# Block 1's words loaded behind the rows of blocks 0 and 1, in a fused attention and expert kernel

## The chip, the cores and the metric

One core of a Trainium2 chip runs the whole program in one launch. The metric is device time in microseconds, the median of several executions. Matmuls run on TensorE, elementwise work on VectorE (DVE in the profile), ScalarE (ACT) and GpSimd (POOL); SyncE (SP) issues most transfers, GpSimd the indirect ones.

## The reference

Three stages, all in float32. An attention with decaying state runs over 4 batches, 8 heads, 768 steps and heads of 48. Its output, as 3072 rows of 384, goes to a layer of 8 experts; each row takes one of them. A dense layer of width 2048 with a squared relu follows.

```python
for t in range(S):
    cur = np.einsum('bhd,bhe->bhde', u[None] * kt, vt)
    y[:, :, t] = np.einsum('bhd,bhde->bhe', rt, state + cur)
    state = wt[:, :, :, None] * state + np.einsum('bhd,bhe->bhde', kt, vt)
...
e_idx = np.argmax(x @ w_gate, axis=1)
for e in range(E):
    mask = e_idx == e
    h = np.maximum(x[mask] @ w1[e], 0.0)
    out[mask] = gate_w[mask, None] * eom[mask, e, None] * (h @ w2[e])
...
g = np.maximum(x @ w_in, 0.0) ** 2
return g @ w_out
```

## The kernel before, in words

The attention works in 16 units (a batch and a pair of heads each). A unit's result `xT` is turned back into rows (`back`, two halves). When a batch is complete, a generator `route_steps` routes its 768 rows in small steps that are woven between other work: logits on TensorE, the choice of an expert on VectorE, ranks, a row `dsi` of destinations, and six indirect scatters by GpSimd that put the rows, sorted by expert within the batch, into the DRAM table `x_rows`. The last batch's steps are the `route_step()` calls. When all is routed, `finish_routing` sorts the experts by their number of rows and sets where each block finds its rows.

The experts' work is cut into blocks of fixed capacity. Block A holds the first 320 rows of expert 0 from the first three batches, so it can start before the last routing. Block 0 holds the rest of expert 0 (128 rows). Blocks 1 to 7 hold the other experts, the fullest first (480, 440, ... rows). A block gathers its rows (`gather`, one indirect DMA of GpSimd for each 128), multiplies them by the gate (`scale`), turns them (`prep_x`), and then goes through eight steps `f` of `up(f)` and `down(f)`. Every float32 factor is split into a high and a low part, and each product takes three matmuls. `prep_w(f)` splits step f's slices of `w1` and `w2` (the words): the high part by ScalarE, the low part by VectorE or GpSimd. The words come in two halves of four steps, 768 KB each for `w1r` and `w2r`, by `load(0)` and `load(1)` on SP, into two buffers that all blocks share. `put_ids` writes the rows' token numbers, 4 bytes each, into the DRAM list `x2_ids`; `put` and `put_A` write a block's result. `convert_load` fetches words of the dense layer, which VectorE converts (`convert_1`, `convert_2`).

Inside a `manual_schedule` each of the named engines keeps the written order. Two such parts stand one behind the other before the branch, and a planner may interleave them; a third stands behind the branch, in which GpSimd's order is the planner's. The branch (`tc.If(rare > 0)`, line 939) leads to work for inputs that the fast path can't hold; here it isn't taken, but each engine waits there for the transfers that it has under way.

What the change touches, in order of time: the end of the attention (`prep_x` of block A and the last unit's `back`), the steps of block A before the branch (`prep_w(FA)`, where FA = 4 is its fifth step, and `prep_w(FA + 1)`), block 1's `load(0)`, issued before the branch, and behind the branch the order of block 0's and 1's gathers, `put_ids`, loads and `convert_load(0)`. Block 0 works with block A's words. Lines 334 and 336 are the high and low parts of the splits, 330 and 331 those of `up`, 341 to 343 the three matmuls, 397 the gather, 242 the scatter, 477 and 481 `put_ids`, 321 and 322 the loads of words, 427 the transposes of `prep_x`.

Of the kernel before, what the change touches and what calls it, by code (L numbers as in the profile page):

```python
# [9 lines left out]
F32 = mybir.dt.float32  # L10
# [11 lines left out]
def rwkv_moe_kernel(  # L22
# [15 lines left out]
    nc = tc.nc  # L38
    B, H, S, D = r.shape
    NT, DM = out.shape  # L40
    E, _, F = w1.shape
# [6 lines left out]
    KD = DM // 128  # L48
# [4 lines left out]
    FA = 4  # L53
# [262 lines left out]
    rawctx = ExitStack()  # L316
    raw = rawctx.enter_context(tc.tile_pool(name="raw", bufs=2))

    def load_expert(pool, w1e, w2e, hf, into=None):
        t, t2 = into or (pool.tile([128, KD, F // 2], F32, name="w1r"), pool.tile([128, KF // 2, DM], F32, name="w2r"))  # L320
        nc.sync.dma_start(t, w1e.rearrange("o (c p) f -> p (o c) f", p=128)[:, :, hf * (F // 2):(hf + 1) * (F // 2)])
        nc.sync.dma_start(t2, w2e.rearrange("o (c p) d -> p (o c) d", p=128)[:, hf * (KF // 2):(hf + 1) * (KF // 2)])
        return t, t2
# [43 lines left out]
    class Block:  # L367
# [14 lines left out]
        def rows(self, i):  # L382
            return min(128, self.cap - 128 * i)

        def words_of(self, e):
            self.w1e, self.w2e = (t[ds(e, 1)] for t in (w1, w2))

        def load(self, hf, again=False):
            self.w1r[hf], self.w2r[hf] = load_expert(self.P.raw, self.w1e, self.w2e, hf, (self.w1r[hf], self.w2r[hf]) if again else None)

        def gather(self, tiles=None):
            one = self.nt == 1
# [5 lines left out]
                                             in_offset=IndirectOffsetOnAxis(ap=self.gcol(n, i), axis=0))  # L398

        def scale(self, eng=None):  # L400

            if self.ids is None:
                self.ids = self.P.xb[0].tile([128, NTL], F32, name="xid", bufs=3)
            for i in range(self.nt):
                n = self.rows(i)
                x, gate = self.xg[:n, i, :DM], self.xg[:n, i, DM:DM + 1]
                if eng:
                    eng.tensor_scalar(x, x, gate, None, op0=ALU.mult)
                else:
                    nc.scalar.activation(x, x, AF.Copy, scale=gate)  # L410
            i, n = divmod(self.cap, 128)
            for ids, num in ([(self.ids[:, :i], self.xg[:, :i, DM + 1])] if i else []) + \
                            ([(self.ids[:n, i:i + 1], self.xg[:n, i, DM + 1:DM + 2])] if n else []):
                if eng:
                    eng.tensor_copy(ids, num)
                else:
                    nc.scalar.copy(ids, num)
# [130 lines left out]
    def block_of(P, k, e):  # L548
        we = [t[e:e + 1] if isinstance(e, int) else t[ds(e, 1)] for t in (w1, w2)]
        return Block(P, CAPS[k], *we, lambda n, i: gi[:n, k, i:i + 1], (k + 1) % 2)  # L550
# [4 lines left out]
    def column(t, k):  # L555
        return nc.values_load(t[0:1, k:k + 1], engines=(ET.SP,), min_val=0, max_val=NCOL - 128 if t is offA else NT)

    def expert_of(k):
        return nc.values_load(bei[0:1, k:k + 1], engines=(ET.SP,), min_val=0, max_val=E - 1)
# [10 lines left out]
    def route_step():  # L570
        return next(routing[B - 1], 0)

    with ExitStack() as actx:
# [302 lines left out]

        blkA = first["A"]
        blkA.ps_w, blkA.w_names = ps_t, ["pt"] * KD
        blkA.prep_x(0)
        route_step()  # L880
        blkA.prep_x(1)
        blkA.prep_x(2)
        route_step()
        units[-1].back(0)
        units[-1].back(1)
        vs = cst.tile([128, 1], F32, name="vs")
        nc.vector.tensor_reduce(vs, viol, axis=AX.X, op=ALU.add)
        pf = ps_t.tile([128, 512], F32, name="pt")
# [6 lines left out]
    def put_ids_A():  # L895
        own = []
        for i in range(blkA.nt):
            n = blkA.rows(i)
            ins = nc.sync.dma_start(x2_ids[ds(column(offA, i) if i else 0, n)], blkA.ids[:n, i:i + 1])
            for o in own:  # L900
                tc.declare_no_dep(ins.ins, o.ins, reason="columns of their own")
            own.append(ins)

    with tc.manual_schedule(engines={ET.PE, ET.DVE, ET.Activation, ET.SP, ET.Pool}):
        put_ids_A()
        route_step()
        route_step()
        blkA.up(0)
        route_step()
        route_step()  # L910
        route_step()
        blkA.prep_w(FA, nc.vector)
        blkA.up(1)
        nc.vector.tensor_scalar(flag[:, 0:1], pf[:1, :1], 0.0, None, op0=ALU.is_le)
        blkA.down(0)
        more = None
        while more is None:
            nc.gpsimd.memset(warm, 0.0)
            more = route_step()
        tc.mark_branch_hint_location("rare", "LikelyTaken", [ET.PE, ET.DVE, ET.SP])  # L920
        finish = finish_routing()
        next(finish)
        blkA.prep_w(FA + 1, nc.vector)
        for f in range(2, FA):
            blkA.up(f)
            if f == 2:
                next(finish)
                next(finish)
                blk1 = block_of(P, 1, expert_of(1))
                blk1.load(0)  # L930
            blkA.down(f - 1)
        for _ in finish:
            pass
        blkA.down(FA - 1)
# [4 lines left out]
    with tc.If(rare > 0, label="rare"):  # L939
        fine = nc.values_load(flag[0:1, 0:1], min_val=0, max_val=1)  # L940
        with tc.If(fine == 0):
# [57 lines left out]
                    route(b, xT, xr, fk, ps_x, True)  # L999
            for _ in finish_routing():  # L1000
                pass
            blk1.words_of(expert_of(1))
            blk1.load(0, True)
            blkA.ps_w, blkA.w_names = ps_x, ["px"] * KD
            blkA.again(FA)
            put_ids_A()
# [61 lines left out]
    def convert_load(n):  # L1068
        f, which = divmod(n, 2)
        q = cv.tile([128, KD, 128, 2], I32, name="cq", bufs=3)  # L1070
        if which == 0:
            nc.sync.dma_start(q.rearrange("p c f o -> p c (f o)"),
                              w_in32.rearrange("(c p) f -> p c f", p=128)[:, :, f * 256:(f + 1) * 256])
        else:
            nc.sync.dma_start(q.rearrange("p c f o -> p (c f o)"), w_out32[f * 128:(f + 1) * 128])
        converted[n] = [q.rearrange("p c f o -> p (c f) o")]
# [117 lines left out]

    with tc.manual_schedule(engines={ET.PE, ET.DVE, ET.Activation, ET.SP}):
        block_rows()
        blocks = [block_of(P, 0, 0), blk1]
        blk0 = blocks[0]
        blk0.w1t, blk0.w2t = blkA.w1t, blkA.w2t
        blk0.gather()  # L1200
        atA = [column(offA, i) if i else 0 for i in range(blkA.nt)]
        blk0.banks(1)
        for f in range(FA, KF):
            blkA.up(f)
            if f + 2 < KF:
                blkA.prep_w(f + 2, nc.vector)
            if f > FA:
                blkA.down(f - 1)
            if f == FA + 1:
                for k in range(1, E):  # L1210
                    if k == 1:
                        blk1.words_of(expert_of(k))
                    else:
                        blocks.append(block_of(P, k, expert_of(k)))
                    blocks[k].banks((k + 1) % 2)
                blk0.put_ids(lambda: column(off, 0))
                blocks[1].load(1)
                convert_load(0)
            if f == KF - 1:
                blk0.prep_x(0)  # L1220
        blocks[1].gather()
        blkA.down(KF - 1)
        blkA.evac()
        for c in range(1, KD):
# [14 lines left out]
        blk0.turn(0)  # L1239
        for f in range(2):  # L1240
            blocks[1].prep_w1(f)
        blocks[1].put_ids(lambda: column(off, 1))
        put_A(1)
        convert_load(1)
        put_A(2)
# [130 lines left out]
```

## Time and profile before

| | |
|---|---|
| time, median of 3 runs | 860.0 us (858.92 to 861.44) |
| the profiled execution | 866.6 us, its span 864.6 us |
| mean granted TensorE clock | 0.984 |
| busy share of the span | PE 95%, PEld 86%, DVE 63%, ACT 43%, POOL 40% |
| DMA | 102.84 MB, mean 119 GB/s |
| PEclk in 40 slices of 21.6 us | 9999999989899999999999999999999999999998 |

All times below count from the start of the span. A line of a timeline has its start, its length, the engine, the line of the kernel, the operation and what it writes and reads; in brackets stands how long the engine was idle before it and what ended that. A busy engine is not one at its peak, and idle time of an engine that nothing waits for costs nothing.

### The profile page before, as it was taken

How to read it: one execution, taken by the hardware profiler on the slowest of the kernel's cores; microseconds unless marked ns; L12 is line 12 of the kernel's file. 1: busy time of each engine (PE TensorE's matmuls, PEld its weight loads, DVE VectorE, ACT ScalarE, POOL GpSimd, SP SyncE). 2: the span in 40 equal slices, each digit the busy share in tenths (PEclk: the TensorE clock that was granted, in tenths of full speed). 3: DMA queues.
4: the chain of work that ended last, by engine and by line, in shares of the span. 5: the costliest groups of instructions: out<-in, count | busy, mean ns of one | idle time of the engine just before them, and what ended most of it. 6: DMA issues, size and time to landing. Idle time of an engine off the chain costs nothing.

```text
span 864.6 us, 14650 instructions
## 1 busy us (share of the span) xinstructions
PE 823.4 (95%) x5484; PEld 742.6 (86%) x5484; DVE 541.0 (63%) x962; ACT 374.5 (43%) x789; POOL 346.0 (40%) x374
## 2 busy tenths in 40 slices
PE   5999999999799999989999999999999999999995
PEld 5888887878688999989998999888898999998994
DVE  7777878877268679768833688788733434344342
ACT  4565555643254554544545334434333333333321
POOL 6564666643345355535465233243310122122111
PEclk9999999989899999999999999999999999999998
DMA  8665567613875677667745222323014033032010
GB/s 174 124 127 111 122 147 205 172 52 131 159 168 165 201 188 194 177 213 213 148 135 180 74 74 92 118 85 109 29 45 138 1 110 101 9 110 66 9 46 36
DMA packets 157359, 102.84 MB, mean 119 GB/s; under 512 B 112348, under 2 KB 140940, under 8 KB 157284
## 3 DMA queue, kind: packets, MB, share of 16 engines
q1 hardware_dynamic: 149044, 86.55, 37.7%
q0 software_dynamic: 4912, 14.65, 5.9%
q10 hardware_dynamic: 3328, 0.66, 0.4%
q8 instruction: 44, 0.72, 0.4%
q14 instruction: 31, 0.25, 0.1%
HBM read 79.34 MB, written 22.50 MB: 118 GB/s over the span
## 4 chain that ended last, share of the span: by engine, by line
PE 66%; DVE 12%; issue 8%; DMA 5%; ACT 4%; POOL 4%; POOLq 0%; DVEq 0%; SPq 0%; ACTq 0%
PE ph L341 9%; PE ph L342 9%; PE ph L343 9%; PE px L343 5%; PE po L341 5%; PE px L341 5%; PE po L342 4%; PE px L342 4%; PE po L343 4%; PE pt L651 3%; PE pa L723 2%; DMA x_rows<-xr,dsi 2%; DMA xg<-x_rows,gi 2%; PE py L754 2%; ACT A L725 1%
## 5 line engine op out<-in xcount | busy, mean ns | idle before, releaser
L1149 DVE SCALAR_TENSOR_TENSOR gg<-ph,rl 128x512 f32<-128x512 f32 x96 | 66.2, 689 | 120.6 <-ACT rl L1147 120.6
L1147 ACT ACTIVATE rl<-ph 128x512 f32<-128x512 f32 x96 | 57.4, 598 | 144.1 <-PE ph L343 144.1
L336 DVE TENSOR_TENSOR gl<-gg,gh 128x512 fp32r<-128x512 f32 x96 | 67.0, 698 | 65.9 <-ACT gh L334 41.9
L334 ACT CAST gh<-gg 128x512 fp32r<-128x512 f32 x96 | 59.6, 621 | 102.7 <-DVE gg L1149 102.7
L336 POOL TENSOR_TENSOR w1l<-w1r,w1h 128x384 fp32r<-128x384 f32 x56 | 59.4, 1068 | 73.1 <-ACT w1h L334 72.8
L330 ACT ACTIVATE hh<-ph 128x320 fp32r<-128x320 f32 (+7 forms) x64 | 32.4, 507 | 117.4 <-PE ph L343 116.0
L336 DVE TENSOR_TENSOR w2l<-w2r,w2h 128x384 fp32r<-128x384 f32 x64 | 63.7, 996 | 18.8 <-ACT w2h L334 18.2
L1095 POOL TENSOR_TENSOR caf<-caf,cbf 128x384 f32<-128x384 f32 x32 | 32.5, 1015 | 104.0 <-DVE cbf L1094 104.0
L331 DVE SCALAR_TENSOR_TENSOR hl<-ph,hh 128x320 fp32r<-128x320 f32 (+7 forms) x64 | 36.7, 574 | 37.3 <-ACT hh L330 37.3
L1173 POOL DMA_INDIRECT out_dram<-ob,tokc x24 | 23.4, 975 | 68.2 <-DVE ob L1172 64.2
L725 ACT COPY A<-pa 128x384 f32<-128x384 f32 x64 | 27.5, 481 | 51.7 <-PE pa L723 51.7
L342 PE MATMUL po<-hl,w2h 128*128 128x320 f32 (+4 forms) x120 | 42.5, 355 | 3.9 <-DVE hl L331 3.9
L726 POOL TENSOR_SCALAR_AFFINE_SELECT A<-A 128x768 f32<-128x768 f32 x32 | 27.9, 871 | 44.3 <-ACT A L725 44.1
L341 PE MATMUL po<-hh,w2h 128*128 128x320 f32 (+4 forms) x120 | 43.2, 360 | 0.0
L343 PE MATMUL po<-hh,w2l 128*128 128x320 f32 (+4 forms) x120 | 42.1, 351 | 0.0
L397 POOL DMA_INDIRECT xg<-x_rows,gi x28 | 28.1, 1004 | 30.4 <-PE po L427 11.9
L671 DVE TENSOR_TENSOR_SCAN suf<-zw,s 128x388 f32<-128x388 f32 x30 | 28.8, 960 | 16.7 <-PE zw L657 16.7
L336 POOL TENSOR_TENSOR x22l<-x2r,x22h 128x512 fp32r<-128x512 f32 x12 | 15.5, 1293 | 51.5 <-ACT x22h L334 51.5
L336 POOL TENSOR_TENSOR x21l<-x2r,x21h 128x512 fp32r<-128x512 f32 x12 | 15.5, 1295 | 45.5 <-ACT x21h L334 45.5
L334 ACT CAST w2h<-w2r 128x384 fp32r<-128x384 f32 x64 | 32.9, 515 | 0.0
L242 POOL DMA_INDIRECT x_rows<-xr,dsi x24 | 24.8, 1035 | 19.8 <-ACT w2h L334 13.1
L334 ACT CAST w1h<-w1r 128x384 fp32r<-128x384 f32 x64 | 32.6, 511 | 0.0
(827 smaller groups left out, 2626.7 us busy)
## 6 DMA issues: line engine op xcount, KB each, us to landing
w1r<-in_moe_w_dram SPq DMA_DIRECT2D x16, 768.0 KB, 6.9
w2r<-in_moe_w_dram SPq DMA_DIRECT2D x16, 768.0 KB, 7.9
x2r<-x_cols SPq DMA_DIRECT2D x12, 768.0 KB, 5.4
cq<-in_moe_w_in_dram SPq DMA_DIRECT2D x16, 384.0 KB, 3.5
cq<-in_moe_w_out_dram SPq DMA_DIRECT2D x16, 384.0 KB, 3.3
vN<-in_v_dram SPq DMA_DIRECT2D x32, 144.0 KB, 3.2
part<-ob SPq DMA_DIRECT2D x24, 192.0 KB, 1.9
ob<-part SPq DMA_DIRECT2D x24, 192.0 KB, 2.4
```

The lines of the kernel that those rows point to most:

```text
L330: nc.scalar.activation(hi, src, AF.Relu)
L331: nc.vector.scalar_tensor_tensor(lo, src, 0.0, hi.bitcast(F32), op0=ALU.max, op1=ALU.subtract)
L334: nc.scalar.copy(hi, src)
L336: lo_eng.tensor_tensor(lo, src, hi.bitcast(F32), op=ALU.subtract)
L341: nc.tensor.matmul(out_, a_of(ah), b_of(bh), start=start, stop=False)
L342: nc.tensor.matmul(out_, a_of(ah), b_of(bl), start=False, stop=False)
L343: nc.tensor.matmul(out_, a_of(al), b_of(bh), start=False, stop=stop)
L671: nc.vector.tensor_tensor_scan(out=self.suf[:, at:at + HL + 1][:, ::-1], data0=z[:, ::-1], data1=s_1[:, ::-1], initial=0.0, op0=ALU.mult, ...
L725: nc.scalar.copy(A[:, :, j], pa[j])
L1095: nc.gpsimd.tensor_tensor(af, af, bf, op=ALU.add)
L1147: nc.scalar.activation(rl, ph, AF.Relu)
L1149: nc.vector.scalar_tensor_tensor(gg, ph, 0.0, rl, op0=ALU.max, op1=ALU.mult)
```

## The change

Ahead of the branch: the last unit's `back(0)` and the routing's second step go before block A's first `prep_x`, and `back(1)` behind it. The fifth step's splits go from behind the routing's VectorE steps to ahead of them. The low part of the sixth step's `w2` goes behind the branch, and so does `load(0)` of block 1, whose repetition in the rare branch is dropped.

Behind the branch: both blocks' gathers come first. `keep_ids`, formerly the end of `scale`, copies block 1's token numbers on GpSimd as soon as its rows are there. SP then issues `put_ids` of block 0, `put_ids` of block 1, `load(0)` and `load(1)`, in this order, at the first step behind the branch. `convert_load(0)` comes later.

```diff
     def scale(self, eng=None):
-        if self.ids is None:
-            self.ids = self.P.xb[0].tile([128, NTL], F32, name="xid", bufs=3)
...
+        if self.ids is None:
+            self.keep_ids(eng)
+
+    def keep_ids(self, eng=None):
+        self.ids = self.P.xb[0].tile([128, NTL], F32, name="xid", bufs=3)
...
+        units[-1].back(0)
+        route_step()
         blkA.prep_x(0)
+        units[-1].back(1)
+        blkA.prep_x(1)
         route_step()
-        blkA.prep_x(1)
         blkA.prep_x(2)
-        route_step()
-        units[-1].back(0)
-        units[-1].back(1)
...
         put_ids_A()
+        blkA.prep_w(FA, nc.vector)
         route_step()
...
-        blkA.prep_w(FA, nc.vector)
         blkA.up(1)
...
-        blkA.prep_w(FA + 1, nc.vector)
+        blkA.prep_w1(FA + 1, nc.vector)
+        blkA.prep_w2(FA + 1, part="hi")
...
-                blk1 = block_of(P, 1, expert_of(1))
-                blk1.load(0)
...
         blk0.gather()
+        for k in range(1, E):
+            blocks.append(block_of(P, k, expert_of(k)))
+            blocks[k].banks((k + 1) % 2)
+        blocks[1].gather()
+        blocks[1].keep_ids(nc.gpsimd)
...
-            if f == FA + 1:
-                for k in range(1, E):
...
+            if f == FA:
+                blkA.prep_w2(FA + 1, nc.vector, part="lo")
                 blk0.put_ids(lambda: column(off, 0))
+                blocks[1].put_ids(lambda: column(off, 1))
+                blocks[1].load(0)
                 blocks[1].load(1)
-                convert_load(0)
...
-        blocks[1].gather()
...
         for f in range(2):
             blocks[1].prep_w1(f)
-        blocks[1].put_ids(lambda: column(off, 1))
+        convert_load(0)
         put_A(1)
         convert_load(1)
```

## Rows read from the trace of the kernel before

**Rows 1.** Chain of waits: start, length, what held it.
```profile
216.22 3.18 DMA xg<-x_rows,gi
...
220.04 0.95 POOL xg L397
...
221.29 10.03 DMA xg<-x_rows,gi
```

**Rows 2.** Timeline of TensorE, 219 to 240 us.
```profile
219.44 0.45 PE L427 MATMUL px<-ident,xg 128*128 128x128 f32 x1 [2.36 <-DMA xg<-x_rows,gi]
...
231.82 0.30 PE L427 MATMUL po<-ident,xg 96*128 96x96 f32 x1 [4.02 <-DVE xg L408]
...
237.21 0.44 PE L341 MATMUL px<-w2h,hh 128*128 128x384 f32 x1
...
239.77 0.38 PE L341 MATMUL ph<-x0h,w1h 128*128 128x480 f32 x1
```

**Rows 3.** DMA issues of single moments: size, us from issue to landing; then all `w1r`.
```profile
w2r<-in_moe_w_dram SPq DMA_DIRECT2D x1, 768.0 KB, 8.2
x_rows<-xr,dsi POOLq DMA_INDIRECT x1, 8.9
...
x_rows<-xr,dsi POOLq DMA_INDIRECT x6, 3.5
...
xg<-x_rows,gi POOLq DMA_INDIRECT x1, 3.1
...
w1r<-in_moe_w_dram SPq DMA_DIRECT2D x1, 768.0 KB, 10.9
...
xg<-x_rows,gi POOLq DMA_INDIRECT x1, 7.2
...
DMA to landing us min/median/max: 5.1/6.9/10.9
```

**Rows 4.** Timeline of SP's DMA issues, 205 to 234 us.
```profile
205.91 0.40 SPq L322 DMA_DIRECT2D w2r<-in_moe_w_dram  x1
...
220.90 0.57 SPq L477 DMA_DIRECT2D x_ids<-xg  x1
221.74 0.41 SPq L321 DMA_DIRECT2D w1r<-in_moe_w_dram  x1
...
231.87 0.40 SPq L477 DMA_DIRECT2D x_ids<-xid  x1
233.09 0.35 SPq L481 DMA_DIRECT2D x_ids<-xid  x1
```

**Rows 5.** Stretches behind an id write: busy time by engine, PEclk, DMA share, GB/s.
```profile
301.00:303.00 2.00, 2.00 (x11) 1.89 (x11) 1.82 (x4) 1.25 (x3) 1.54 (x2) 1.00 0.70 25
...
309.00:311.00 2.00, 2.00 (x13) 1.99 (x12) 1.97 (x4) 0.44 (x2) 1.45 (x2) 1.00 1.04 403
```

**Rows 6.** Timeline of VectorE, 197 to 207 us.
```profile
197.74 0.17 DVE L229 CAST dsi<-dst 128x6 int32<-128x6 f32 x1
197.82 0.55 DVE L336 TENSOR_TENSOR w1l<-w1r,w1h 128x384 fp32r<-128x384 f32 x1
...
205.92 0.15 DVE L303 SCALAR_TENSOR_TENSOR flag<-flag 1x1 int32<-1x1 int32 x1
```

**Rows 7.** Stretches at half clock, columns as in rows 5.
```profile
188.80:195.60 6.80, 6.80 (x30) 5.67 (x28) 3.39 (x14) 3.40 (x11) 0.00 (x0) 0.50 0.02 0
...
233.20:236.60 3.40, 3.40 (x14) 3.30 (x13) 0.21 (x1) 0.03 (x1) 0.00 (x0) 0.50 1.37 253
```

**Rows 8.** SP's waits, 200 to 232 us: total, times, longest.
```profile
SPq L939 <- SPq L939: 6.7, 2, 3.5
...
SPq L477 <- DMA x_ids<-xg: 2.4, 1, 2.4
```

**Rows 9.** Timeline of ScalarE, 228 to 237 us.
```profile
228.04 0.94 ACT L334 CAST w1h<-w1r 128x384 fp32r<-128x384 f32 x2
...
236.57 0.58 ACT L334 CAST hh<-px 128x512 fp32r<-128x512 f32 x1 [3.85 <-PE px L500]
```

More of the change, by code (lines that the diff above doesn't have):

```diff
@@ L317, in rwkv_moe_kernel, with load_expert @@
     raw = rawctx.enter_context(tc.tile_pool(name="raw", bufs=2))
-    def load_expert(pool, w1e, w2e, hf, into=None):
-        t, t2 = into or (pool.tile([128, KD, F // 2], F32, name="w1r"), pool.tile([128, KF // 2, DM], F32, name="w2r"))
+    def load_expert(pool, w1e, w2e, hf):
+        t, t2 = pool.tile([128, KD, F // 2], F32, name="w1r"), pool.tile([128, KF // 2, DM], F32, name="w2r")
         nc.sync.dma_start(t, w1e.rearrange("o (c p) f -> p (o c) f", p=128)[:, :, hf * (F // 2):(hf + 1) * (F // 2)])
@@ L383, in rows, with load @@
             return min(128, self.cap - 128 * i)
[L385 to L389, printed above, removed]
+        def load(self, hf):
+            self.w1r[hf], self.w2r[hf] = load_expert(self.P.raw, self.w1e, self.w2e, hf)
         def gather(self, tiles=None):
@@ L1001, in rwkv_moe_kernel @@
                 pass
-            blk1.words_of(expert_of(1))
-            blk1.load(0, True)
             blkA.ps_w, blkA.w_names = ps_x, ["px"] * KD
@@ L1196, in rwkv_moe_kernel @@
         block_rows()
-        blocks = [block_of(P, 0, 0), blk1]
+        blocks = [block_of(P, 0, 0)]
         blk0 = blocks[0]
@@ L1208, in rwkv_moe_kernel @@
                 blkA.down(f - 1)
-            if f == FA + 1:
-                for k in range(1, E):
[L1211 to L1215, printed above, removed]
+            if f == FA:
+                blkA.prep_w2(FA + 1, nc.vector, part="lo")
                 blk0.put_ids(lambda: column(off, 0))
+                blocks[1].put_ids(lambda: column(off, 1))
+                blocks[1].load(0)
                 blocks[1].load(1)
-                convert_load(0)
             if f == KF - 1:
                 blk0.prep_x(0)
-        blocks[1].gather()
         blkA.down(KF - 1)
```

## The prediction

> **What bounds the kernel now.** I read the page first: TensorE is busy for 95% of the span at a clock of 0.984, so only stretches in which it stands still or runs at half clock can give time back. Two of the three slices in which the page gives a clock digit of 8 lie between 173 and 238 us, and there the change works. I then read the chain of waits there and, beside it, one timeline per engine.
>
> The chain [rows 1] is the reader's key. From about 198 to 231.4 us it hardly touches TensorE: it goes through the last routing's six scatters into `x_rows`, the gather of block 0 (216.22) and the last of block 1's four gathers (221.29). TensorE shows the ends of the two long transfers as two stalls, 2.36 us before 219.44 and 4.02 us before 231.82, and starts block 1 at 239.77 [rows 2]. I call that moment U; from U on the page's slices show TensorE at 9 with hardly an exception, so the kernel's end moves one for one with U.
>
> Two transfers are late, and not for the same reason. The last scatter needs 8.9 us where the six have a median of 3.5 [rows 3]; block 1's first words, issued on SP beside it, take 8.2 us in the same moment. Those are what the change takes away. The last gather needs 10.0 us where the one 1.25 us earlier needed 3.1 [rows 1, 3]. The words of `load(1)` are issued after it, at 221.74 [rows 4], so they look guilty. But I looked at every other place where `put_ids` writes its 4-byte elements to `x2_ids` with transfers behind it: each of the seven times little moves for the next 7 to 8 us. The clearest: the ids of block 3 go out around 300 us, then 25 GB/s from 301 to 303 with almost only gathers in flight, and 403 GB/s again from 309 to 311 [rows 5]. A gather issued at 301.15, with no words behind it, took 7.2 us [rows 3]. So I take it that the id write at 220.90 [rows 4] holds up the last gather and the words behind it (10.9 us for `w1r` [rows 3]). I call this the hold.
>
> **The change part by part.** Times are those of the profiled execution (866.6 us, 864.6 of them span; the median of three unprofiled runs is 860.0). I carry one sum for U and add the difference to 860.0.
>
> 1. *Last unit turned back sooner.* One `back` and the routing's last six matmuls move into TensorE's waits for `xg`; no instruction is added. What they free, and what the fifth step's splits add ahead of the routing on VectorE (two lo parts, 0.55 us each [rows 6], and two ScalarE casts before them), oppose each other. Worst: the lo parts stand right in front of the routing's first reduction, which eats the gain and a little more, -0.3. Best: they fall into VectorE's waits between `x0`, `x1` and `x2`, and some of TensorE's 6.8 us at half clock there goes [rows 7], about 2.4 in all. I take 1.2, about half way, as no row is nearer to one end. The destination rows `dsi` are then ready at 196.7 instead of 197.9 (197.74 + 0.17).
>
> 2. *Scatters.* The last is issued 7.5 us after `dsi` (205.4). At the median of 3.5 us it lands at 207.7, before at 214.3; one us either way is my bound. POOL then needs 1.9 us to its first gather (214.3 to 216.22 [rows 1]): block 0's gather at 209.6, block 1's last one 5.07 later at 214.7. That is 6.6 us earlier than before, and the first stall on TensorE (2.36) goes.
>
> 3. *SP behind the branch.* Before, SP stood in the branch's join until the words had landed (205.91 + 8.2 = 214.1; one half of its 6.7 us of waits there [rows 8]), then took 6.8 us for ten register loads and the issue of block 0's ids at 220.90. VectorE's flag came at 206.07 (205.92 + 0.15); it loses 1.2 from part 1, and 0.93 and 0.47 for the splits that leave its queue: 203.5. From there the branch, the other wait of SP's there (none to 3.5 us), and the loads with the issue take 7.8 to 11.3, so 211.3 to 214.8; block 0's rows (209.6 + 3.2) must be there first. So ids 0 go out between 212.9 and 214.8, at or before the last gather. Before they stood 0.4 ahead of the gather that took 10.0 and 0.9 behind the one that took 3.1. So I expect the last gather to be caught again. Without words beside it I give it 8.5 us, between 7.2 (the lone one) and 10.0: block 1's rows land at 223.2 (221.9 to 224.7), before at 231.3.
>
> 4. *`keep_ids` on POOL, then ids 1, then the words.* Two small copies on POOL; no row shows such a copy there, so I bound them by 0 and by 2.0 (two of the page's 1.0 us operations of POOL on 128x384) and take 0.6, since they are three columns wide. Ids 1 go out at 224.0, their second part 1.2 later (231.87 and 233.09 [rows 4]), and only then `w1r` at 225.9 and `w2r` at 226.5. The new wait therefore has all four loads, block A's result and the conversions queued behind it on SP. SP also waits before ids 1 until ids 0 have landed [rows 8], before about 7.4 us after their issue (2.4 us of waiting behind the issues in between), so 220.3 to 222.2; so even an undisturbed gather brings ids 1 hardly below 220.3.
>
> 5. *The words in their own hold.* Before, `load(0)` had landed at 214 and ScalarE split it at 228.04 without waiting. Now the words stand right behind 480 four-byte writes. The nearest row is the `w1r` of `load(1)`, issued 0.84 us behind ids 0: 10.9 us. So `w1r` is there at 236.8, `w2r` at 238.8 (768 KB at the 403 GB/s behind a hold [rows 5]). Ends for `w1r`: 231.0 at the shortest landing of any `w1r`, 5.1 us [rows 3], were there no hold, and 239 if the 480 elements hold 2 us longer than the 128 did.
>
> 6. *From the words to U.* ScalarE's queue is in order: two `w1h` (0.94), `x0h` and then the `hh` of the second turn (0.58 each, priced by the one `hh`) [rows 9]. TensorE's second `down_rows` waits for that: 238.9. It took 2.56 us (237.21 to 239.77) at full clock. But TensorE will have stood still since about 227.5 (its work up to there is finished 4 us sooner), some 11 us. After the 4.02 us stall it was granted half clock (0.50, 1.2 GHz) for 3.4 us [rows 7]; so I take 3.3 us, between 2.56 and twice that, and U = 242.2.
>
> 7. *Moved at no cost:* the lo part of step 6's `w2` goes behind the branch, where VectorE had more than 1 us free per step (hidden by `up`, 0.5 us if not); `convert_load(0)` is needed only at about U + 5; the dropped reload in the rare branch is not executed.
>
> Sum: U 239.8 to 242.2, **+2.4 us**: 8.1 us won on block 1's rows and 10.5 lost by making its words wait for them. Time 860.0 + 2.4 = **862.4** (a profiled execution: 869.0). With part 1 at -0.3 or 2.4 (±1.3), the gather at 7.2 or 10.0 (±1.4), the words ±2 and the clock ±1, taken as independent, the likeliest case reaches from 859.5 to 865.5.
>
> **A rule of the skill, weighed.** The Trainium skill ("DMA: Bandwidth & Descriptors", section "Why small descriptors are slow") gives small descriptors a fixed overhead of a few cycles and 32 bytes each; by that 480 of them over 16 engines would be over in a fraction of a microsecond and hold up nobody, the words would land undisturbed, and the sum would be that of the first rival. The rows on the hold speak against it. The same page ("Rules for kernel authors") advises to issue a DMA early and wait late; this change does the opposite for `load(0)`, which here was wholly hidden.
>
> **Rivals.**
> - *The words are not held (faster).* The id writes are not what stops the transfers, or they stop only what is already in flight. Then `w1r` lands at 231.0 and U = 231.0 + 2.1 + 3.3 = 236.4, -3.4: 856.6. With the last gather free as well, ids 1 at 220.3 and U near 233: 853. For it: the 368 writes at 188 to 191 us met no transfer, so one case is unseen. Against it: the gather that was alone [rows 3], the stretch behind block 3's ids [rows 5] and the other holds. It decides from a landing of `w1r` below 8 us.
> - *The holds are there, but everything before them is earlier.* Part 1 gives 2.4 and ids 0 leave at once, at 211.7; ids 1 leave when ids 0 have landed, at 219.1, and the words land at 231.9: U = 237.3, -2.5: 857.5. For it: TensorE's half-clock stretch around the routing might go. Against it: the gather would have to be caught for less than the shortest 7.2.
> - *Holds add up (clearly slower).* The words come only after 13 us (480 elements instead of 128, and two parts), and conversions behind them reach VectorE late: U = 245, +5: 865.
> - *Nothing to see.* The gain on the rows and the loss on the words cancel within a microsecond or two: 859 to 862. That the change isn't in the program as written is not a case I see: its loads and waits stand in queues in written order.
>
> **How the numbers follow.** About 0.3%, 2.6 us, is what a measurement of this kernel can tell from no change. Forecast (holds as computed, +0.5 to +4.5): 0.41; holds add up: 0.12; cancels (-2 to +0.5): 0.15; everything earlier: 0.14; words not held: 0.18. The forecast lies on the line between no change and slower, so I divide its 0.41 into 0.20 and 0.21; everything earlier lies on the other line, 0.07 and 0.07. Slower 0.21 + 0.12 = 0.33; same 0.20 + 0.15 + 0.07 = 0.42; faster 0.07 + 0.18 = 0.25. For 8 times in 10 the range takes in the earlier case, the upper part of the first rival and the added holds: 855.0 to 866.0.
>
> **What would show it.** After: the last scatter lands about 3.5 us after its issue; no stall before block 0's first transposition; block 1's last gather still needs 7 us or more and the ids of block 0 leave within 1 us of it; `w1r` of block 1 takes about 11 us from issue to landing, some 20 us later than now; TensorE stands still for about 11 us before the second `down_rows`, and ScalarE's `w1h` is what it waits for behind a DMA. Wrong if `w1r` lands in 5 us or `load(0)` is issued before 221 us.

## The result, and the profile after

The changed kernel takes **870.75 us** (median of five runs, 868.46 to 871.72) where the kernel before took 861.13 beside it: 1.0115 times as long, 95% interval 1.0097 to 1.0132. In a second comparison (below) it was 869.61, ratio 1.0092 (1.0063 to 1.0122). Forecast were 862.4, at most 866. One of the five runs of before beside the first result took 1608 us; why is not known; the median counts it, the ratio leaves it out.

| | before, as shown | after |
|---|---|---|
| profiled execution, us | 866.6 | 868.46 |
| span, us | 864.6 | 866.6 |
| block 1 starts on TensorE (U), us | 239.8 | 241.7 |

The two profiles differ by 1.9 us at U and by 2.0 at the end, close to the +2.4 of the forecast. The timed runs differ by 8 to 10. So the first thing to learn is in this table: the pair of profiles says one thing, the runs another.

The chain of waits after, answering to [rows 1] (start, length, what held it):

```profile
201.42 8.65 DMA x_rows<-xr,dsi
...
211.06 0.99 POOL xg L394
...
214.98 7.96 DMA xg<-x_rows,gi
...
223.09 0.35 POOL xid L414
223.46 0.42 SPq L476
...
224.75 0.36 SPq L480
225.35 10.29 DMA w1r<-in_moe_w_dram
235.69 0.39 issue
236.09 0.51 ACT w1h L334
236.59 0.46 ACT x0h L334
237.05 0.50 ACT hh L334
237.59 0.69 PE px L341
```

Read from the top, it is the forecast's list: scatters, early gathers, a gather that needs 8 us (the last but one; the last, issued at 216.24, needs 7.6), the copy of the ids on POOL, the ids, and the words, which come 10.3 us after their issue with ScalarE and TensorE right behind them. SP's issues, answering to [rows 4]:

```profile
214.59 0.04 SPq L476 DMA_DIRECT2D x_ids<-xg  x1
223.46 0.42 SPq L476 DMA_DIRECT2D x_ids<-xid  x1
224.75 0.36 SPq L480 DMA_DIRECT2D x_ids<-xid  x1
225.35 0.43 SPq L321 DMA_DIRECT2D w1r<-in_moe_w_dram  x1
...
227.19 5.58 SPq L322 DMA_DIRECT2D w2r<-in_moe_w_dram  x1
```

The last line is new: this one issue takes 5.58 us, SP itself is held up. The stretches behind the two id writes, answering to [rows 5] (same columns; the last is GB/s):

```profile
218.00:220.00 2.00, 1.67 (x10) 1.17 (x9) 0.69 (x2) 0.59 (x2) 0.00 (x0) 1.00 0.86 38
220.00:222.00 2.00, 2.00 (x14) 1.71 (x13) 0.86 (x3) 1.19 (x4) 0.00 (x0) 1.00 0.41 44
...
228.00:230.00 2.00, 2.00 (x17) 1.97 (x16) 0.00 (x0) 0.00 (x0) 0.00 (x0) 1.00 0.29 34
230.00:232.00 2.00, 0.57 (x6) 0.35 (x4) 0.00 (x0) 0.00 (x0) 0.00 (x0) 1.00 0.28 37
232.00:234.00 2.00, 0.00 (x0) 0.00 (x0) 0.00 (x0) 0.00 (x0) 0.00 (x0) 1.00 0.83 194
```

With four loads of 768 KB issued from 225.35 on, 34 to 37 GB/s move from 228 to 232. TensorE's timeline, answering to [rows 2]:

```profile
237.59 0.69 PE L341 MATMUL px<-w2h,hh 128*128 128x384 f32 x1 [7.02 <-ACT hh L334]
...
241.67 0.38 PE L341 MATMUL ph<-x0h,w1h 128*128 128x480 f32 x1
```

ScalarE's, answering to [rows 9], shows what it waited for:

```profile
235.67 0.92 ACT L334 CAST w1h<-w1r 128x384 fp32r<-128x384 f32 x2 [9.17 <-DMA w1r<-in_moe_w_dram]
```

Behind the stall TensorE worked at half clock again (0.51, the lower of its two levels, 1.2 GHz), for four microseconds (to [rows 7]):

```profile
237.60:241.60 4.00, 4.00 (x12) 3.70 (x13) 2.50 (x6) 2.31 (x6) 3.24 (x4) 0.51 1.07 382
```

### The profile page after: what moved, and what is told of

It is laid out like the page before. It is cut to its first block, busy times and chain, and to the rows that moved or that the text cites. A ratio compares the mean times of both kernels' runs of the same rounds, so it can differ in the third digit from the quotient of the medians.

```text
span 866.6 us, 14644 instructions
## 1 busy us (share of the span) xinstructions
PE 821.0 (95%) x5484; PEld 739.8 (85%) x5484; DVE 538.5 (62%) x960; ACT 374.0 (43%) x789; POOL 346.7 (40%) x376
## 4 chain that ended last, share of the span: by engine, by line
PE 58%; DVE 19%; issue 9%; ACT 5%; DMA 5%; POOL 3%; SPq 0%; POOLq 0%; DVEq 0%; ACTq 0%
PE ph L342 7%; PE ph L341 7%; PE ph L343 7%; PE px L341 4%; PE px L343 4%; PE px L342 4%; PE po L341 4%; PE po L342 4%; PE po L343 4%; PE pt L650 3%; PE pa L722 3%; DVE gg L1145 3%; ACT gh L334 2%; DVE ca L1079 2%; DVE gl L336 2%
## 5 line engine op out<-in xcount | busy, mean ns | idle before, releaser
L336 POOL TENSOR_TENSOR x20l<-x2r,x20h 128x512 fp32r<-128x512 f32 x12 | 15.5, 1290 | 41.2 <-ACT x20h L334 41.2
```

The costliest lines, as they stand in the source:

```text
L336: lo_eng.tensor_tensor(lo, src, hi.bitcast(F32), op=ALU.subtract)
```

## The experiments

Theory A: the hold is real, and the profiled execution of before was an unusual one, whose last gather was caught by it; most runs of before are not caught, so they start block 1 some 6 us sooner than its profile shows, and the forecast compared with the wrong execution. Rivals: profiling makes each execution longer (B); the difference lies in stalls far behind (C); the words are late for another reason than the ids in front of them; the loss is in the prologue.

**The kernel before again, four more profiles** (`c0_before`, `c1_before`, `c2_before`, `c3_before`; no edit).

> The kernel before, unchanged, for a second profiled execution of it. The first one took 866.6 us, its timed runs 858.9 to 861.4. Theory A (the profiled execution was an unusual one: its last gather was caught by the hold behind block 0's ids, and in most executions it is not): this profile shows no stall of 4 us before 231.8, block 1 starting on TensorE (U) near 233 to 235, and a time near 860; caught again, it shows 866 and U near 239.8. Theory B (the profile lengthens every execution alike, by some 6 us): this profile shows U near 239.8, the 4 us stall, a time near 866, and so do the profiles of all other kernels against their own timed runs. Theory C (the difference lies in the stalls far behind the change, 2.4 us near 372 us in the profile of before): U near 239.8 and no stall there.

> The kernel before once more, for a third profiled execution. Theory A: if block 0's ids go out over 1 us behind the last gather, it lands in 3 to 4 us and the execution takes 857 to 861; if they go out before it or within 0.2 us, it needs 8 to 10 us and the execution takes 863 to 868.

> The kernel before, for a fourth profiled execution. The first three: 866.6 with the ids 0.4 us ahead of the last gather, 858.6 with them 1.1 behind, 862.8 with them 3.8 behind but the scatters 1.1 later and a further stall at 243. Theory A: caught (ids ahead of or within 0.2 us of the gather) 864 to 868, not caught 857 to 863.

> The kernel before, for a fifth profiled execution. So far ids 0 behind the last gather by -0.4, 1.1, 3.8 and 2.5 us gave landings of 10.0, 3.0, 4.6 and 3.7 us and 866.6, 858.6, 862.8 and 861.0 us. Theory A: a landing over 7 us only if the ids lie less than 0.3 us behind the gather or ahead of it.

| profile of before | ids 0 behind last gather, us | gather needs, us | U | time |
|---|---|---|---|---|
| the one shown | -0.39 | 10.0 | 239.8 | 866.6 |
| c0 | 1.14 | 3.0 | 232.0 | 858.6 |
| c1 | 3.80 | at most 4.7 | 233.4 | 862.8 |
| c2 | 2.48 | at most 3.7 | 236.2 | 861.0 |
| c3 | 2.61 | at most 3.5 | 232.8 | 864.8 |

The second and third column come from rows like these, of c0. POOL's timeline has the last gather:

```profile
219.58 0.94 POOL L397 DMA_INDIRECT xg<-x_rows,gi  x1 [0.30 <-issue]
```

SP's timeline has the ids 1.14 us behind it:

```profile
220.72 0.57 SPq L477 DMA_DIRECT2D x_ids<-xg  x1
```

and VectorE's has the first use of the rows, 3.0 us behind the gather's issue:

```profile
222.60 0.42 DVE L408 TENSOR_SCALAR xg<-xg 96x384 f32<-96x384 f32 x1 [0.59 <-DMA xg<-x_rows,gi]
```

The same kernel that stood still for 2.36 and 4.02 us [rows 2] starts block 1 at 232.0 here, with neither stall. One execution of five was caught, the one that was shown. Its first stall, behind the late last scatter, is missing in the four others as well, so the race is not the whole difference in U. B falls (c0's profile is faster than its runs' median, 862.17), and C: the 2.6 us stall near 370 is in c0 too. The four others took 861.8 on average, as the timed runs do (861.1 to 863.6 in the six comparisons).

c1 missed its band (862.8 for 857 to 861), and c3, at 864.8, lies above the 863 given with c2 for executions that aren't caught. In both VectorE waits on a line that reads `cq`, the words of the later conversion, and TensorE waits for VectorE. In c3 (2.63 and 1.24 us in c1):

```profile
241.18 0.36 DVE L1082 TENSOR_SCALAR ca<-cq 128x384 int32<-128x384 int32 x1 [3.20 <-DMA x_ids<-xid]
243.14 0.49 PE L342 MATMUL po<-hl,w2h 128*128 128x480 f32 x1 [1.78 <-DVE hl L331]
```

The profile puts VectorE's wait down to the landing of block 1's ids. So where the gather is free, the ids can still cost something further on, and the race is not all of before's spread (857 to 866 in eleven of c0's twelve runs).

**Ids behind the words** (`e1_ids_behind_words`: the changed kernel, both id writes moved).

```
             if f == FA:
...
-                blk0.put_ids(lambda: column(off, 0))
-                blocks[1].put_ids(lambda: column(off, 1))
                 blocks[1].load(0)
                 blocks[1].load(1)
...
         put_A(2)
+        blk0.put_ids(lambda: column(off, 0))
+        blocks[1].put_ids(lambda: column(off, 1))
         blocks[1].prep_x(0)
```

> The changed kernel, with the ids of blocks 0 and 1 written only behind the third part of block A's result, so that load(0) and load(1) go out with no 4-byte writes ahead of them. If these writes hold up the words (the theory of the prediction): w1r, issued near 214 to 225, lands in 5 to 7 us instead of 10.3, the last gather lands within 4 us instead of 7.9, TensorE's stall ahead of the second down_rows goes, U near 231 to 233 instead of 242, the time near 860 to 862 instead of 870.8. Rival (the words are late because SP issues them late or because of the gathers in flight): w1r still needs 10 us, U and time as in the changed kernel, within 2 us. A third outcome: the front is earlier, but the holds now fall on block 2's first words and TensorE waits for these instead; then U near 232 and the time above 865.

854.34 us, 0.9893 of before (0.9866 to 0.992): faster than both kernels. U is 227.1; the stall of 7.02 is gone, one of 1.18 is left:

```profile
220.71 0.30 PE L426 MATMUL po<-ident,xg 96*128 96x96 f32 x1 [1.18 <-DVE xg L402]
```

Moving two lines takes 15 to 16 us off the changed kernel (870.75 and 869.61). The hold theory expected 860 to 862: it counted only the wait of the words, and not that everything behind the branch comes sooner too. Some 2.5 us of the 14.6 at U are an earlier front (first scatter at 196.05, in the changed kernel 198.53), which varies from execution to execution, see below. The words of `load(0)` landed in 5.4 us, as expected; the last gather needed 6.5, not the 4 expected, beside the words of both loads. A gather can so be slow without ids ahead of it.

**Is it the 4-byte elements?** (`d1_probe_column`, `d2_probe_row`, `d3_probe_64B`, `d4_probe_512B`: e1 with one transfer that computes nothing ahead of `load(0)`.)

```
+    probe = dram.tile([128, 1], F32, name="probe")      # d2: [1, 128]  d3: [128, 16]  d4: [128, 128]
...
+                nc.sync.dma_start(probe, ident[:, 0:1])  # d2: ident[0:1, 0:128]  d3: ident[:, 0:16]  d4: ident[:, 0:128]
                 blocks[1].load(0)
```

> Kernel e1 (changed kernel, ids behind block A's result) with one transfer added that computes nothing: one column of the identity, 128 elements of 4 bytes from 128 partitions, is written to a scratch tensor right ahead of load(0). If 4-byte writes hold up whatever stands behind them: w1r, which needed about 8 us there, needs 13 to 17, gathers in flight too, and the time is 3 to 7 us over e1 (854.3). Rival (SP's waits or the gathers make the words late): no change from e1.

> As d1_probe_column, with the same 512 bytes written as one row from one partition (one element of 512 bytes instead of 128 of 4). If the number of small elements makes the hold: no stretch of 7 us with little traffic behind it, time within 1.5 us of e1 (854.3). Rival (any write to HBM at this place holds the reads behind it): like d1, 3 to 7 us over e1.

> As d1_probe_column (860.6, last gather 11 us late), with 16 columns of the identity instead of one: still 128 elements from 128 partitions, each of 64 bytes instead of 4. If the number of elements or partitions makes the hold: as d1, block 1's rows near 227 and about 860. If the 4 bytes make it: rows near 220, no stretch of little traffic from 211 on, about 854. Something between, if the hold shrinks with the size of the element.

> As d3_probe_64B, with the whole identity: 128 elements of 512 bytes, 64 KB. If the number of elements or partitions makes the hold: as d1, about 860. If small elements make it: rows near 220, about 854, at most the fraction of a microsecond more that 64 KB take at the 370 to 400 GB/s seen there.

d1 took 860.55 us, d2 853.48, e1 854.34: 128 elements of 4 bytes cost 6 to 7 us, the same 512 bytes in one element nothing. d3 took 857.56 and d4 858.77, between the two, so here the stretches decide (GB/s last; the probe goes out at 208.99 in d1, 208.90 in d2, 212.77 in d3). d1:

```profile
212.00:214.00 2.00, 0.80 (x6) 0.54 (x4) 0.47 (x1) 0.00 (x0) 1.39 (x3) 1.00 0.71 41
214.00:216.00 2.00, 0.00 (x0) 0.00 (x0) 0.00 (x0) 0.00 (x0) 0.53 (x1) 0.75 0.39 52
216.00:218.00 2.00, 0.00 (x0) 0.00 (x0) 0.00 (x0) 0.00 (x0) 0.00 (x0) 0.50 0.57 45
218.00:220.00 2.00, 0.59 (x3) 0.59 (x4) 0.00 (x0) 0.08 (x1) 0.00 (x0) 0.50 0.33 48
220.00:222.00 2.00, 2.00 (x9) 2.00 (x9) 0.77 (x2) 0.62 (x2) 0.00 (x0) 0.50 0.99 364
```

d2:

```profile
213.00:215.00 2.00, 2.00 (x15) 1.75 (x14) 0.93 (x3) 1.35 (x5) 1.42 (x2) 1.00 1.08 410
```

and d3:

```profile
213.00:215.00 2.00, 2.00 (x16) 2.00 (x15) 0.62 (x2) 0.44 (x1) 1.70 (x2) 1.00 0.56 110
215.00:217.00 2.00, 2.00 (x16) 2.00 (x15) 0.49 (x1) 0.44 (x1) 1.39 (x3) 1.00 0.83 273
217.00:219.00 2.00, 2.00 (x16) 1.97 (x15) 0.68 (x2) 0.70 (x3) 0.73 (x1) 1.00 1.04 397
```

In d1 41 to 52 GB/s move until 220, eleven microseconds behind the probe's issue, and the first `w1r` needs 12.9 us (e1: 5.4); TensorE stands still for 6.6 us and falls to half clock (0.50). In d3 the words run at 397 GB/s four microseconds behind the probe. 64-byte elements from the same 128 partitions make no hold. What d3 and d4 lose against e1 they lose earlier: their first scatter is issued at 198.7 and 199.1 (e1: 196.1), and TensorE waits 3.1 us at 208 where it waited 1.3 at 203 in e1. That makes 4 to 5 us; at U d3 lies 3.8 and d4 6.3 behind e1, so for d4 some 1.5 us stay open. That front varies between executions of one program, see below.

**The prologue alone** (`e3_prologue_only`: before with the new order ahead of the branch), and with `load(1)` ahead of the ids as well (`e5_prologue_load1_first`).

```
-                blk0.put_ids(lambda: column(off, 0))
                 blocks[1].load(1)
+                blk0.put_ids(lambda: column(off, 0))      # e5
```

> The kernel before, with only the orders ahead of the branch changed as in the changed kernel: the last unit turned back between the routing steps, and the fifth step's splits ahead of the last routing. load(0), the ids and block 1's gather stay where they were. The prediction gave this part 1.2 us on the destination rows (bounds -0.3 to 2.4). If the time comes from this part: dsi at 197 or later and 3 to 9 us slower than before. If it is free as predicted: dsi 1 us sooner or the same, and the time within 1.5 us of before; all of the loss is then in what moved behind the branch.

> The kernel before with the orders ahead of the branch changed as in the changed kernel (as in e3_prologue_only), and one line more: load(1) issued ahead of block 0's ids instead of behind them. In e3 the scatters began some 2.8 us sooner than before, but block 0's ids went out 0.10 us behind the last gather, which then took 7.8 us, and the time stayed that of before. If that lost race is where the 2.8 us went: with the ids about 1.3 us later the last gather lands within 4 us, TensorE's wait for it (2.1 us) goes, the second turn stands near 228 instead of 231.4, and the time is 3 to 5 us under e3. Rival (the 2.8 us are no gain, a shift of the attention's end in that one profile): the gather lands soon, but the time stays within 1.5 us of before.

e3: 863.61, ratio 0.9993 (0.9975 to 1.0011). Its scatters start at 195.70 (before 198.69), but SP wrote the ids 0.10 us behind the last gather, which then took 7.8 us. TensorE waits 2.10 us for its rows, and 2.44 for those of block 0, whose gather went out 5 us ahead of the ids: 3 us won ahead of the branch are given back in these two waits, one of them behind the ids. e5: 860.56, 3 us under e3, but beside other runs of before; against those each lies about 1 us from the other (ratios 0.9979 and 0.9993), where 3 to 5 were expected. Its profile doesn't bear the reason out either: with the ids 1.56 us behind it, the gather needed 7.3 us all the same, now beside `load(1)`'s words, while 296 to 371 GB/s were moved from 220 to 226. Inconclusive.

**The prologue where no race hides it** (`e6_e1_old_prologue`: e1 with before's order ahead of the branch).

```
-        units[-1].back(0)
-        route_step()
-        blkA.prep_x(0)
-        units[-1].back(1)
-        blkA.prep_x(1)
-        route_step()
-        blkA.prep_x(2)
+        blkA.prep_x(0)
+        route_step()
+        blkA.prep_x(1)
+        blkA.prep_x(2)
+        route_step()
+        units[-1].back(0)
+        units[-1].back(1)
...
-        blkA.prep_w(FA, nc.vector)                 # goes back behind the fifth route_step
```

> Kernel e1 with the orders ahead of the branch put back as before: the last unit turned back behind the last routing, the fifth step's splits behind it. In e1 no hold and no race stands between the scatters and block 1, so the prologue's part should come out here unmasked. If it is worth the 1.2 us of the prediction, or the 2.5 to 2.8 that the scatters' start shows (195.7 to 196.1 against 198.5 to 199.6): 855.5 to 857. If it is worth nothing, or the scatters' earlier start is only the attention's: 853.5 to 855. If it costs: under 853.

857.09, 2.75 us over e1, or 4.4 if each is set against the runs of before beside it: the prologue's part is worth about that much. The first scatter agrees (198.28 against 196.05), though that start varies by as much between executions of one program, and the runs of the two overlap (855.7 to 860.8 and 852.4 to 857.9).

**Forcing the race both ways** in the kernel before: block 0's ids always late (`e2_before_ids0_late`), always early (`e4_ids0_first`).

```
+                blk0.put_ids(lambda: column(off, 0))      # e4: ahead of the register loads
                 for k in range(1, E):
...
-                blk0.put_ids(lambda: column(off, 0))
...
+        blk0.put_ids(lambda: column(off, 0))              # e2: just ahead of block 1's ids
         blocks[1].put_ids(lambda: column(off, 1))
```

> The kernel before, with only the ids of block 0 written later, just ahead of those of block 1. Nothing is then held at 221 to 230. If the hold of block 0's ids is what caught the last gather: it lands within 4 us of its issue (10.0 in the first profile of before), TensorE's 4.02 us stall goes, U near 234 to 236, and the profiled time agrees with the timed runs. Theory A: the timed runs are within 1.5 us of those of before, since most of them escape the hold anyway. If most of before's executions are caught as in the profile: 3 to 5 us faster than before. Rival (the gather was slow because of the words of load(1) behind it): still 8 to 10 us, no change.

> The kernel before, with one line two lines higher: block 0's ids are written ahead of the register loads for the other blocks' experts instead of behind them, so SP reaches them some microseconds sooner, bound only by the landing of block 0's rows. Theory A (whether the last gather goes out ahead of or behind these ids decides the time of a run of the kernel before): the ids now always go out ahead of the last gather, it always needs 8 to 10 us, the 4 us stall is always there, and the runs lie at 864 to 868 with little spread, where before's run from 857 to 871. Rival (the gather's delay has to do with load(1), or the spread with something else): load(1) also goes out sooner, time as before, 860 to 863, same spread.

e2: 858.67 (0.9949 of before, 0.9922 to 0.9976), the last gather in 4.5 us, U 232.1. e4: 863.29 (1.0014, 0.9987 to 1.004), the rows of the last gather ready 9.8 us after its issue, TensorE's stalls for block 1's rows 3.17 and 1.27 us, U 236.9. In these two profiles the order of ids and gather does what Theory A says.

In time both runs went against it. Since most runs of before escape the hold, e2 was to lie within 1.5 us of before; it lies 4.9 under the 863.55 beside it, which had been written down as the sign that most runs are caught. e4 was to lie at 864 to 868 with little spread; it can't be told from the 861.92 beside it and spreads over 7.5 us (858.2 to 865.7; e2 over 10.4). e2 also takes the hold of block 0's ids off `load(1)` and `cq`, which may cost in executions that aren't caught (c1 and c3), so it doesn't measure the race alone; that was not tested. How many of before's timed runs are caught, and how much of its spread is the race, stays open.

**Which part of the changed kernel loses?** Its order undone one piece at a time: the loads ahead of the ids (`e7_loads_first`), `load(0)` back ahead of the branch (`e8_after_load0_early`), block 1's ids back at their old place (`e9_ids1_old_place`), and the changed kernel itself (`a0_after`).

```
-                blk0.put_ids(lambda: column(off, 0))
-                blocks[1].put_ids(lambda: column(off, 1))      # e9: this line alone
                 blocks[1].load(0)                              # e8: this line alone, to f == 2 ahead of the branch
                 blocks[1].load(1)
+                blk0.put_ids(lambda: column(off, 0))           # e7
+                blocks[1].put_ids(lambda: column(off, 1))      # e7
...
         convert_load(0)
+        blocks[1].put_ids(lambda: column(off, 1))              # e9
         put_A(1)
```

> The changed kernel with two pairs of lines swapped: load(0) and load(1) ahead of the ids of blocks 0 and 1, at the same place of the loop. Nothing else is undone. If the loss is that the words wait for block 1's rows and then stand in the hold of their ids: w1r is issued near 210 and lands by 217, block 1's second turn is no longer waiting for ScalarE's split of it, block 1 starts 10 to 13 us sooner than in the changed kernel (243.6 at its first transpose by L515), time 855 to 860. The ids of block 0 then go out near 213 to 216, so the last gather may still be caught (start 3 us later than in e1). Rival (the words' order is not it, the loss is in the prologue or in keep_ids on POOL): 869 to 871.

> The changed kernel with one part undone: load(0) goes out ahead of the branch again, as before (with the reload in the rare branch, which isn't executed). All else is as changed: the prologue, the early gather, keep_ids on POOL, both ids ahead of load(1). If the words of load(0) behind the ids are where the changed kernel loses: ScalarE has them long before 228, the 7 to 9 us stall ahead of the second down_rows near 238 goes, and what is left is the last gather in the hold of ids 0 (rows near 226 to 228, block 1's second turn near 230 to 232): 860 to 865, some 6 to 9 us under the changed kernel. Rival (the loss is in the holds of both ids ahead of everything, whoever is behind them): another stall of 5 us or more further on, 866 to 870.

> The changed kernel with one line moved: block 1's ids go back to where the kernel before had them, behind the loads and the conversion's first transfer (cq), ahead of the second part of block A's result. Ids 0 stay ahead of the loads. If the place of ids 1 is the loss: load(0) and load(1) go out near 216 to 218 and wait out the hold of ids 0 alone (to about 224), w1r lands near 226 to 228 instead of 235.7, the stall near 238 goes or shrinks under 2 us, the ids' hold near 231 to 240 meets nothing that TensorE waits for, as in the kernel before: 856 to 862. Rival (any hold ahead of the loads is enough): still 5 us of stall or more, 866 to 870.

> The changed kernel, unchanged, for a second profile and more timed runs beside those of the kernel before. Theory A: its order leaves nothing to a race (ids 0 always catch the last gather, the words always stand behind the ids), so the runs lie close together at 868 to 872, and the profile shows again a stall of 5 to 9 us ahead of the second down_rows near 237 and w1r needing 10 us. If its time varies as before's does (over 5 us), the race theory is not what makes before's spread.

| | U | TensorE's stall, for whom | time |
|---|---|---|---|
| after | 241.7 | 7.02 at 237.6, words | 870.75 |
| a0 | 242.2 | 8.72 at 238.3, words | 869.61 |
| e7 | 228.5 | 7.94 at 245.0, `cq` | 865.52 |
| e8 | 234.7 | 6.06 at 249.3, `cq` | 871.24 |
| e9 | 235.8 | 1.95 at 229.4, rows | 863.41 |
| e1 | 227.1 | 1.18 at 220.7, rows | 854.34 |

e7 and e8 both missed their bands (855 to 860 and 860 to 865). In e7 U comes 13 us sooner and the time only 4 to 5. In e8, with the words there in time, U comes 7 us sooner, and the time is that of the changed kernel. The hold of block 1's ids then falls on the next transfer in SP's queue that somebody waits for, `cq`, the first load of the later conversion; VectorE keeps its written order and waits for it, and TensorE waits for VectorE. VectorE's timeline in e7:

```profile
243.02 0.36 DVE L1078 TENSOR_SCALAR ca<-cq 128x384 int32<-128x384 int32 x1 [8.84 <-DMA cq<-in_moe_w_in_dram]
```

and TensorE's, which waits for VectorE:

```profile
244.99 0.77 PE L342 MATMUL po<-hl,w2h 128*128 128x480 f32 x1 [7.94 <-DVE hl L331]
```

The same two in e8. There the profile puts the end of VectorE's wait down to a store (`x_cols<-yT`); that it is `cq` that it waits for is read from the line, which reads it:

```profile
246.67 0.99 DVE L1085 TENSOR_SCALAR ca<-cq 128x384 int32<-128x384 int32 x1 [6.34 <-DMA x_cols<-yT]
249.27 0.77 PE L342 MATMUL po<-hl,w2h 128*128 128x480 f32 x1 [6.06 <-DVE hl L331]
```

e9 puts one line back and wins 6 to 7 us, though it leaves the words behind block 0's ids (U 235.8; 863.41, a little above the band given). So what the changed kernel pays for against the kernel before is that block 1's ids stand ahead of everything that follows; that the words of `load(0)` are the first in line decides only where the stall is seen. From e9 to e1 there are 9 us more, which block 0's ids ahead of the loads, the second place of block 1's ids and the front share; no run separates these. a0's seven runs still spread over 4.8 us, a little more than expected of a kernel that leaves nothing to the race.

## Why the prediction was wrong

The failed step is the base of the sum, in part 3 and in the line that heads the parts: "I carry one sum for U and add the difference to 860.0". The difference was taken against an execution of 866.6 us whose last gather "needed 10.0" [rows 1, 3], and added to the median of timed runs, 860.0. Against its own base the forecast was right: a profiled execution of 869.0 was forecast, and 868.46 measured. Of the 8.4 us between 862.4 and 870.75, 6.6 are this base (866.6 against 860.0) and 2.3 that the profiled execution of the changed kernel was the fastest of its five runs; the forecast itself was 0.5 too high. The four other profiles of before have neither of the two stalls that the sum set out from. The terms:

| term | forecast | measured |
|---|---|---|
| U, changed kernel | 242.2 | 241.7 and 242.2 |
| U, before | 239.8 | 239.8 once; 232.0, 233.4, 236.2, 232.8 |
| difference of U | +2.4 | 241.95 - 233.6 (mean of the four) = +8.3 |
| difference of time | +2.4 | +9.6 and +7.7 |

The "8.1 us won on block 1's rows" are not there in an execution that isn't caught: c0 has the rows at 222.6, the changed kernel at 223.9. What is left is the loss on the words. It could have been seen ahead: the profiled execution lay 5.2 us above the slowest of its three timed runs (861.44), and held two stalls on this path of 6.4 us together, the second decided by 0.4 us between an issue on SP and one on POOL [rows 1, 2, 4]. The prediction noted 866.6 beside 860.0 and, with "a profiled execution: 869.0", took the gap as common to both kernels.

A second premise failed: that "the kernel's end moves one for one with U". From U to the end of the span the four profiles of before take 624.6, 627.4, 622.9 and 629.9 us, the two of the changed kernel 624.9 and 623.6, and e7 and e8 635.3 and 633.1. So the profiled executions of the two kernels differ by 6.3 us (868.1 against 861.8) where U differs by 8.3, and that the 8.3 lies between the timed differences is partly luck.

Step by step, for the changed kernel:

1. Prologue: 1.2 us taken, at most 2.4; e6 measured 2.75 to 4.4 in time. Mis-sized. In the changed kernel's own profile it doesn't show: `dsi` ready at 197.8 instead of 196.7, and a wait of 3.2 us at 207.8 behind VectorE.
2. Scatters and gathers: last scatter issued at 205.23, 7.5 us behind `dsi` (196.7 and 7.5 make 204.2; the 205.4 that stands in part 2 is the kernel before's), landed by 210.1 (207.7), block 0's gather at 211.06 (209.6), the last one at 216.24 (214.7). The gathers are 1.5 us late each. Against the four other profiles of before (block 0's gather at 213.6 to 215.8) the gain is some 3.6 us, not 6.6.
3. Ids 0 at 214.59 (212.9 to 214.8), the last gather caught, rows 7.6 us after the issue (8.5), at 223.9 (223.2). Right.
4. `keep_ids` 0.34 and 0.18 us (0.6); ids 1 at 223.46 and 224.75 (224.0, 225.2); `w1r` at 225.35 (225.9). Right.
5. `w1r` 10.3 us (10.9), landed at 235.6 (236.8). Right, and with it the choice between the rule of the Trainium skill ("DMA: Bandwidth & Descriptors", section "Why small descriptors are slow") and the rows: the words were not undisturbed.
6. ScalarE's chain 1.9 us (2.1); the second `down_rows` 4.1 us (3.3), almost all at half clock; U 241.7 (242.2). Right. TensorE's stall was 7.0 us instead of some 11, as the work ahead of it ended later.

Of the rivals none came true as written. That the hold would have fallen on `cq` had it not fallen on the words (e8) was not foreseen.

## What to carry to other kernels

Before a difference is added to a timed median, ask whether the profiled execution is one of the timed ones: if it lies outside their range, look in it for a wait that hangs on which of two issues comes first, and work out the sum for both outcomes. That a race is on the path doesn't yet say what it costs: lost every time, it could not be told from the kernel before in time (e4). An edit that removes the wait's first victim (e8) wins nothing while the cause stays in front of the queue. Here the cheap cure was to put small writes behind everything that somebody waits for (e1); the probe in d2 suggests writing them as rows instead, which was not tried for the ids themselves.

## What the runs showed of the hardware that was not expected

- One DMA of 128 elements of 4 bytes to HBM holds up the loads that SP issues and the gathers that POOL issues, for 7 to 11 us (c3: 26 to 74 GB/s from 224 to 232 behind the ids at 222.4; d1: 41 to 52 GB/s until 220, 364 from there on). 128 elements of 64 bytes (d3) or 512 bytes (d4: 351 GB/s by 216 to 218, its probe at 213.2) don't, nor does one of 512 bytes (d2: 410 GB/s four microseconds behind it). The Trainium skill ("DMA: Bandwidth & Descriptors", section "Specifications") says that transfers below 512 bytes do a read-modify-write; by these runs that alone is not the hold, as 64 bytes lie below that size too. Where between 4 and 64 bytes it begins was not measured, nor whether it is the size of the element or that the 128 elements of d1 lie side by side within 512 bytes of HBM (those of d3 cover 8 KB).
- While the hold lasts, SP's own issues are slow: one of 5.58 us in the changed kernel, of 7.97 in d1 (the same load in e1, without a hold: 0.43).
- The front varies. The first scatter was issued between 198.5 and 200.5 us in the five profiles of the kernel before, one and the same program; in those with the new order ahead of the branch it was between 195.7 and 199.2. What in the attention ahead makes this difference stays open, and what share of the spread of both kernels it has.
